# Casting loads on the GpSimd queue, one merged multiply for q and k, a shared phase step and a new program order in a gated linear-attention and GEGLU kernel

## The chip, the cores and the metric

The kernel runs on one core of a Trainium2 chip. The metric is the device time of one execution in microseconds; smaller is better. A run is marked slow when it is over 1.5% above the fastest run of the same kernel, else fast, and ratios are the mean time of one kernel's fast runs over the mean time of the other's fast runs of the same rounds, so they are not quite the ratio of the medians that are quoted beside them. The runs were made on several chips of the same kind. The kernel before took 258 us on some of them and 261 to 264 us on others. A ratio from one chip is not compared finely with a ratio from another.

## The reference

Four sequences of 768 steps with 8 heads of width 48 go through a recurrence with a complex decay; its real output, 3072 rows of 384, goes through a gated feed-forward block.

```python
mag = np.sqrt(a_re * a_re + a_im * a_im)
scale = np.minimum(mag, 0.999) / (mag + 1e-06)
a_re_n, a_im_n = (a_re * scale, a_im * scale)
for t in range(S):
    # ar, ai: a_re_n and a_im_n of step t
    new_re = ar * S_re - ai * S_im
    new_im = ar * S_im + ai * S_re
    S_re, S_im = new_re + k_t v_t^T, new_im        # 48 x 48 per head (shortened)
    y[:, :, t] = q_t S_re
# ...
out = (gelu(x @ w_gate) * (x @ w_val)) @ w_out      # x: y as 3072 x 384, d_ff 1536 (shortened)
```

## The kernel before

The kernel works on 24 chunks of 128 steps. Three chunks are a "unit", which is half of a sequence; a unit's a_re and a_im (576 KB each) give logarithm and angle of the decay, TensorE sums them along time, ScalarE makes exponentials (`E`) and sines (`sn`) of the sums. VectorE multiplies q and k by the exponentials (`qe`, `ke`) and by cosine and sine (`qp`, `kp`) into a tile `pair`. This is transposed either on TensorE with a copy (`tp`, `tps`) or by a transposing DMA (`tpd`). Scores, state and output follow, then the feed-forward part: two up products `g` and `v`, Gelu, product, down product `fo`.

The order is written by hand: a plan of some thousand words is executed as program order on every engine. A word such as `ldk3=1` is "load k of chunk 3 into buffer 1". The parts that the change and the argument touch:

```python
        q=bufs("q", 6, [128, H, D], fp32), k=bufs("k", 6, [128, H, D], fp32),
        v=bufs("v", 6, [128, H, D], fp32),
# ...
    def load(nm, i, slot):
        t = take(nm, (nm, i), slot)
        src = DRAM[nm]
        if nm in ("q", "k", "v"):
            b, c = divmod(i, NCH)
            nc.sync.dma_start(out=t, in_=src[b, :, c * L:(c + 1) * L, :].transpose([1, 0, 2]))
            return
# ... a_re and a_im: also on the sync queue
    def load_weight(nm, after):          # "ldwo@v4": not before v of chunk 4 has arrived
        t, src = WEIGHTS[nm]
        if after:
            a = T[after]
            # ...
            nc.gpsimd.tensor_copy(out=t[:, 0, 0:1], in_=a)
        nc.gpsimd.dma_start(out=t, in_=src.rearrange("(c p) f -> p c f", p=128))
# ...
    def ph(c, slot, **_):
        # ...
        nc.vector.tensor_scalar(out=t[:, 1], in0=T["cumt", c],
                                scalar1=TURN / (2.0 * PI), scalar2=None, op0=ALU.mult)
        nc.vector.tensor_scalar(out=t[:, 0], in0=t[:, 1],
                                scalar1=TURN / 4.0, scalar2=None, op0=ALU.add)
# ...
    def ke(c, slot, **_):
        nc.vector.tensor_tensor(out=take("ke", ("ke", c), slot), in0=T["k", c], in1=T["e", c][:, 1],
                                op=ALU.mult)
    # qe: the same with q and T["e", c][:, 0]
    def vb(c, slot, **_):
        nc.gpsimd.tensor_copy(out=take("vb", ("vb", c), slot), in_=T["v", c])
# ...
    def tpd(c, hg, slot, **_):           # transposing DMA of half a pair tile; xtd is the same for x
        src = T["pair", c][:, hg * 4:(hg + 1) * 4].rearrange("p h i s d -> p (h i s d)")
        nc.sync.dma_start_transpose(out=take("tps", ("tps", c, hg), slot), in_=src)
```

## Time and profile before

| | before |
|---|---|
| median of the timed runs | 258.99 us |
| span of the profiled run (slow) | 263.8 us |
| first Gelu, which is the start of the feed-forward part | 44.12 us |
| TensorE busy | 212.6 us |

The prediction shows the busy times, a table by stretches and the pieces of the chain around the output weights. Three more views of the same profile are needed. The first is the share of each engine in the chain that ended last, where "DMA" is time in which the chain waited for a transfer. (The chain is followed back from the last instruction, at each step to what released it.)

```profile
PE 49%; DMA 18%; ACT 16%; DVE 9%; issue 2%; POOL 0%; SPq 0%; DVEq 0%; ACTq 0%
```

The second is the span cut in two at the first Gelu; the columns are the stretch and its length, then the busy time of PE, PEld, DVE, ACT and POOL with the number of instructions, the clock granted to TensorE, the share of the DMA engines and GB/s.

```profile
0.00:44.12 44.12, 18.56 (x157) 12.58 (x158) 28.69 (x49) 29.17 (x38) 10.23 (x34) 0.88 1.01 211
44.12:263.80 219.68, 194.01 (x2878) 163.21 (x2874) 168.86 (x297) 136.60 (x211) 14.53 (x22) 0.97 0.77 143
```

TensorE, the busiest engine, was idle for 44.12 - 18.56 = 25.6 us ahead of the first Gelu and for 219.68 - 194.01 = 25.7 us after it. This run was a slow one. A fast run of 258.66 us has a span of some 256.9 us (the profiled runs' times are 1.7 to 1.8 us above their spans), so with the same busy time the idle time is 256.9 - 212.6 = 44.3 us, and about 19 us of it come after the first Gelu. That is an estimate: it takes the opening to be the same in a fast run, as a fast run of one of the experiments (b_ph, first Gelu at 44.16 us) suggests.

The third is the loads of q, k and v whose transfer fell in the opening (source, queue, number, size of one, median us from issue to landing):

```profile
k<-in_k_dram SPq DMA_DIRECT2D x6, 192.0 KB, 4.0
...
q<-in_q_dram SPq DMA_DIRECT2D x4, 192.0 KB, 3.8
v<-in_v_dram SPq DMA_DIRECT2D x4, 192.0 KB, 8.5
```

There are 14 of them. Over the whole run the landing times to compare with later are these:

```profile
aim<-in_a_im_dram SPq DMA_DIRECT2D x2, 576.0 KB, 7.3
...
tps<-pair SPq DMA_TRANSPOSE x26, 3.8
```

### The profile page before, as it was taken

Reading aid. Unit: us, or ns where it says so; the run is one execution under the profiler, and the core shown is the slowest. Engines: PE = TensorE matmul, PEld = TensorE weight load, DVE = VectorE, ACT = ScalarE, POOL = GpSimd, SP = SyncE. Lnnn points to the kernel's source line nnn. Section 1 sums busy time; section 2 is a strip of 40 time slices with the busy share of each in tenths; the row PEclk is TensorE's granted clock in tenths of the full one; section 3 lists DMA queues with packets and bytes.
Section 4 is the critical chain, followed back from the end, with each engine's and each line's share of the span. In section 5 each row is a group of like instructions: output and inputs, shape, how many; then the busy total and the mean of one; then the engine's idle time right before and its main releaser. Section 6 shows DMA issues by size and latency. Waiting matters only on the chain.

```text
span 263.8 us, 7255 instructions
## 1 busy us (share of the span) xinstructions
PE 212.6 (81%) x3031; PEld 175.8 (67%) x3031; DVE 197.6 (75%) x346; ACT 165.8 (63%) x248; POOL 24.8 (9%) x56
## 2 busy tenths in 40 slices
PE   0043678991974989978897898999998999899994
PEld 0021268991542779755787788986667978888962
DVE  4671897976399699999994676789999966854441
ACT  3859738466299576999962333989999523332500
POOL 8100202120000012100020001000100000000000
PEclk9999759998698699999999999999999999999999
DMA  7999998999199999489899999299913968861102
GB/s 215 268 211 205 188 208 172 178 190 171 44 198 232 183 215 191 106 174 211 175 142 170 175 162 188 59 171 219 141 46 103 151 117 193 108 58 47 47 31 89
DMA packets 156017, 40.61 MB, mean 154 GB/s; under 512 B 146512, under 2 KB 155216, under 8 KB 155984
## 3 DMA queue, kind: packets, MB, share of 16 engines
q1 hardware_dynamic: 153632, 36.62, 72.8%
q0 software_dynamic: 2352, 3.54, 7.9%
q8 instruction: 23, 0.38, 0.6%
q14 instruction: 10, 0.08, 0.1%
HBM read 30.67 MB, written 4.72 MB: 134 GB/s over the span
## 4 chain that ended last, share of the span: by engine, by line
PE 49%; DMA 18%; ACT 16%; DVE 9%; issue 2%; POOL 0%; SPq 0%; DVEq 0%; ACTq 0%
PE bank L404 23%; PE bank L427 14%; DMA tps<-pair 10%; DMA wo<-in_moe_w_out_dram 5%; PE bank L289 5%; PE bank L356 3%; ACT e L299 3%; ACT th L278 3%; ACT L445 2%; ACT e L300 2%; PE bank L342 2%; DMA v<-in_v_dram 2%; ACT cs L311 2%; DVE pair L326 2%; ACT tps L212 2%
## 5 line engine op out<-in xcount | busy, mean ns | idle before, releaser
L414 ACT ACTIVATE gel<-bank 128x512 bf16<-128x512 f32 x72 | 42.1, 598 | 51.5 <-PE bank L404 36.9
L420 DVE TENSOR_TENSOR h<-bank,gel 128x512 bf16<-128x512 f32 x72 | 48.2, 686 | 12.9 <-PE bank L404 10.8
L404 PE MATMUL bank<-xt,wg 128*128 128x128 bf16 x864 | 57.0, 221 | 0.3 <-DMA xt<-x 0.3
L427 PE MATMUL bank<-wo,h 128*128 128x384 bf16 x288 | 52.3, 334 | 5.3 <-DMA wo<-in_moe_w_out_dram 5.3
L404 PE MATMUL bank<-xt,wv 128*128 128x128 bf16 x864 | 56.2, 219 | 0.4 <-ACT gel L414 0.4
L404 PEld LDWEIGHTS <-wg 128*128 128x128 bf16 x864 | 51.0, 99 | 1.4 <-issue 0.7
L404 PEld LDWEIGHTS <-wv 128*128 128x128 bf16 x864 | 50.2, 98 | 0.8 <-issue 0.5
L427 PEld LDWEIGHTS <-h 128*128 128x128 bf16 x288 | 27.5, 100 | 22.4 <-DMA wo<-in_moe_w_out_dram 5.4
L359 DVE TENSOR_TENSOR ssb<-bank,tri 128x512 bf16<-128x512 f32 x48 | 32.3, 684 | 11.9 <-PE bank L356 11.7
L323 POOL CAST vb<-v 128x384 bf16<-128x384 f32 x24 | 15.3, 642 | 161.3 <-DMA v<-in_v_dram 101.5
L356 PE MATMUL bank<-tps 128*128 128x128 bf16 x192 | 18.9, 225 | 7.2 <-DMA tps<-pair 5.0
L311 ACT ACTIVATE cs<-ph 128x768 bf16<-128x768 int16 x24 | 19.4, 848 | 4.7 <-DVE ph L306 4.6
L289 PEld LDWEIGHTS <-cum 128*128 128x128 bf16 x36 | 4.5, 124 | 25.5 <-issue 22.9
L356 PEld LDWEIGHTS <-tps 128*128 128x128 bf16 x192 | 12.2, 100 | 10.9 <-DMA tps<-pair 5.8
L445 ACT ACT_TABLE_LOAD x14 | 18.0, 1283 | 1.0 <-PEq L471 0.8
L304 DVE TENSOR_SCALAR ph<-bank 128x384 int32<-128x384 f32 x24 | 13.3, 552 | 7.1 <-PE bank L289 7.1
L289 PE MATMUL bank<-lx,cum 128*128 128x384 bf16 x18 | 4.7, 422 | 16.7 <-DVE lx L275 16.7
L372 PE MATMUL bank<-vb,ssb 128*128 128x48 bf16 x192 | 14.9, 183 | 1.5 <-DVE ssb L359 1.5
L342 PE MATMUL bank<-ident,pair 128*128 128x128 bf16 x176 | 14.1, 234 | 2.1 <-DVE pair L326 2.1
L326 DVE TENSOR_TENSOR pair<-ke,cs 128x768 bf16<-128x768 bf16 x24 | 12.9, 553 | 2.5 <-DMA tps<-pair 2.5
L212 DVE COPY o<-bank 128x384 f32<-128x384 f32 x10 | 5.6, 557 | 12.1 <-PE bank L427 12.1
L299 ACT ACTIVATE e<-bank 128x384 bf16<-128x384 f32 x24 | 12.6, 527 | 3.0 <-PE bank L289 2.9
(70 smaller groups left out, 298.1 us busy)
## 6 DMA issues: line engine op xcount, KB each, us to landing
k<-in_k_dram SPq DMA_DIRECT2D x24, 192.0 KB, 3.8
q<-in_q_dram SPq DMA_DIRECT2D x24, 192.0 KB, 3.7
v<-in_v_dram SPq DMA_DIRECT2D x24, 192.0 KB, 4.1
out_dram<-o SPq DMA_DIRECT2D x24, 192.0 KB, 2.1
are<-in_a_re_dram SPq DMA_DIRECT2D x18, 192.0 KB, 3.7
aim<-in_a_im_dram SPq DMA_DIRECT2D x18, 192.0 KB, 3.8
are<-in_a_re_dram SPq DMA_DIRECT2D x2, 576.0 KB, 5.2
aim<-in_a_im_dram SPq DMA_DIRECT2D x2, 576.0 KB, 7.3
```

Of the source, the lines that this page charges most:

```text
L289: nc.tensor.matmul(ps, mat, xin[:, :, c2, :], start=(n == 0), stop=(n == len(srcs) - 1))
L299: act(out=e[:, 1], in_=T["cum", c], func=AF.Exp, scale=-0.5)
L311: act(out=take("cs", ("cs", c), slot).rearrange("p s h d -> p (s h d)"), in_=lo[:, :, 0], func=AF.Sin, scale=2.0 * PI / TURN)
L326: nc.vector.tensor_tensor(out=T["pair", c][:, :, i, :, 0:D], in0=e.unsqueeze(2).to_broadcast([128, H, 2, D]), in1=T["cs", c].rearrange("p ...
L342: nc.tensor.transpose(ps[:, 2 * hi + i, :], T["pair", c][:, hg * 4 + hi, i], ident)
L356: nc.tensor.matmul(ps[:, hi, :], t[:, 2 * hi + 1, :], t[:, 2 * hi, :], start=True, stop=True)
L359: nc.vector.tensor_tensor(out=take("ssb", ("ssb", c, hg), slot), in0=T["sc", c, hg], in1=tri.unsqueeze(1).to_broadcast([128, 4, 128]), op= ...
L404: nc.tensor.matmul(ps[:, fi * L:(fi + 1) * L], w[:, i, fc * 128:(fc + 1) * 128], T["xt", c][:, i, :], start=(i == 0), stop=(i == NDM - 1))
L414: act(out=take("gel", ("gel", c, f), slot).rearrange("p a t -> p (a t)"), in_=T["g", c, f], func=AF.Gelu)
L420: nc.vector.tensor_tensor(out=T["h", c][:, f * FW:(f + 1) * FW, :].rearrange("p a t -> p (a t)"), in0=T["v", c, f], in1=T["gel", c, f].rea ...
L427: nc.tensor.matmul(ps, T["h", c][:, fc, :], wo_sb[:, fc, :], start=(fc == 0), stop=(fc == NFF - 1))
L445: nc.scalar.preload_act_table_set(TABLES[word[4:]])
```

## The change

The intent is to take work from VectorE, which was full in part of the middle. q, k and v are cast to bf16 by the DMA itself, so that the multiply by the decay runs on bf16 operands, and q and k share one tile and one multiply. The first half of the phase step can run on ScalarE. GpSimd's casts of v go away. The order is new as well: the plan is rewritten from end to end, with five contiguous units instead of two, three units instead of two that take the other form of the logarithm step (SQUARES in the kernel), and more transposing DMAs (36 of pairs for 26, 17 of x for 15).

```diff
-FAST = (0, 1,)
+FAST = (0, 1, 2, 3, 4,)
-        q=bufs("q", 6, [128, H, D], fp32), k=bufs("k", 6, [128, H, D], fp32),
-        v=bufs("v", 6, [128, H, D], fp32),
+        qk=bufs("qk", 8, [128, 2, H, D], bf16), v=bufs("v", 12, [128, H, D], bf16),
...
-            nc.sync.dma_start(out=t, in_=src[b, :, c * L:(c + 1) * L, :].transpose([1, 0, 2]))
+            for n, a in enumerate(src):                  # src: (q, k) or (v,)
+                nc.gpsimd.dma_start(out=t[:, n] if nm == "qk" else t,
+                                    in_=a[b, :, c * L:(c + 1) * L, :].transpose([1, 0, 2]))
...
-    def load_weight(nm, after):
-        ...                                             # the wait for another tile
+    def load_weight(nm):                                # the weights wait for nothing
...
+        if eng == "A":                                  # ph, 14 of 24 times
+            act(out=t[:, 1], in_=T["cumt", c], func=AF.Copy, scale=TURN / (2.0 * PI))
...
-    ke, qe (two multiplies, fp32 input), vb (cast of v on GpSimd)
+    def qk(c, slot, **_):
+        nc.vector.tensor_tensor(out=take("qke", ("qke", c), slot), in0=T["qk", c], in1=T["e", c],
+                                op=ALU.mult)
```

(The lines with "ke, qe" and the comments are shortened; the plan's diff is left out.)

## The prediction

> **What bounds the kernel now.** I read the page's busy shares first, then busy time by stretch, then the chain that ended last, then the groups and DMA issues. The profiled run is of the slow kind (263.8 us of span, granted clock 0.955; the timed runs have a median of 258.99), so I use it for durations and order, and take some microseconds off absolute times.
>
> ```profile
> PE 212.6 (81%) x3031; PEld 175.8 (67%) x3031; DVE 197.6 (75%) x346; ACT 165.8 (63%) x248; POOL 24.8 (9%) x56
> ```
>
> TensorE is the busiest engine, VectorE second, and POOL nearly free. The stretches (span, then busy PE, PEld, DVE, ACT, POOL, clock, DMA share, GB/s) say where TensorE is not fed:
>
> ```profile
> 0.00:12.00 12.00, 0.00 (x0) 0.10 (x1) 5.99 (x10) 7.86 (x7) 6.85 (x28) 1.00 0.93 245
> 12.00:30.00 18.00, 9.05 (x35) 4.35 (x35) 10.27 (x16) 12.82 (x21) 1.55 (x3) 0.91 1.06 208
> 44.00:66.00 22.00, 15.90 (x323) 15.52 (x321) 17.25 (x30) 13.11 (x19) 3.25 (x5) 0.94 1.04 180
> 66.00:90.00 24.00, 18.95 (x141) 11.33 (x142) 16.66 (x30) 17.63 (x27) 0.51 (x1) 0.78 0.81 165
> 90.00:132.00 42.00, 37.21 (x570) 31.69 (x569) 41.07 (x74) 37.04 (x52) 5.32 (x9) 0.99 0.88 178
> 170.00:200.00 30.00, 30.00 (x351) 22.22 (x348) 28.51 (x52) 28.29 (x44) 1.69 (x2) 1.00 0.79 142
> 230.00:264.00 34.00, 30.16 (x434) 25.24 (x431) 14.91 (x24) 8.49 (x15) 0.00 (x0) 1.00 0.25 53
> ```
>
> Three kinds of time: an opening of some 44 us in which the feed-forward matmuls can't start; stretches where VectorE is full (41.07 of 42 us); and an end where TensorE alone works. The DMA engines are at 0.8 to 1.06 until about 200 us. In order of time the chain has these pieces:
>
> ```profile
> 46.78 5.09 DMA v<-in_v_dram
> 51.92 0.72 POOL vb L323
> ...
> 53.40 12.48 DMA wo<-in_moe_w_out_dram
> 65.93 4.04 PE bank L427 x12
> ```
>
> So the output weights were held until chunk 4's v had landed and been cast; TensorE then stood still for 5 us and ran its first output group cold (4.04 us, where later ones take 1.95).
>
> **What the Trainium skill says.** "VectorE: DVE Perf Modes", section on the perf-mode tier table: a tensor_tensor runs at 2x only if every tensor is 16-bit in SBUF, else at 1x. The trace agrees: half the elements with an fp32 input take the same time as twice as many in bf16.
>
> ```profile
> L319 DVE TENSOR_TENSOR qe<-q,e 128x384 bf16<-128x384 f32 x24 | 12.7, 551 | 1.9 <-DMA q<-in_q_dram 1.7 <-ACT e L300 0.2
> L326 DVE TENSOR_TENSOR pair<-ke,cs 128x768 bf16<-128x768 bf16 x24 | 12.9, 553 | 2.5 <-DMA tps<-pair 2.5
> ```
>
> "DMA: Bandwidth & Descriptors", section "SWDGE vs HWDGE vs iDMA": a DMA that casts must come from GpSimd, whose cores write its descriptors. The trace has three such DMAs, the weights; they kept POOL 0.79 to 1.06 us each. Same page, "Issuing engines are not separate DMA queues": all queues share the 16 DMA engines. The trace agrees: the two queues' shares add to 1.06 in 12 to 30 us. "SBUF — State Buffer", section "SBUF: two separate sides": VectorE in a two-port mode locks GpSimd out, so descriptors wait. Nothing in this trace shows that; only the short second phase step and the clamp are candidates, so I give it little.
>
> **The change part by part.** "Spacing" below is start to start when back to back, read from the timeline.
>
> VectorE. The 48 multiplies of k and q at 0.465 us spacing (22.3 us) become 24 of 128x768 in bf16, taken at the 0.465 us of the pair multiply: minus 11.1. Of 24 phase steps 14 go to ScalarE: minus about 8. The new plan has 7 transposed-tile copies instead of 15 (0.6 us): minus 4.8. More output, state and x copies (44 for 30, 0.465 us): plus 6.5. The rest (x transposes, logarithm units) cancels. VectorE falls from 187 to about 170 us of spacings.
>
> ScalarE. 14 phase steps at 0.37 us: plus 5.2. One more table load: plus 1.3. Two tile copies (0.9) and 12 narrow copies (0.37) fewer: minus 6.2. It stays at 154 us.
>
> TensorE. 80 transposes of pairs and 6 of x go (0.056 us each): minus 4.8. Five instead of two (batch, half) units use the three-matmul cumulative sums: 18 more at 0.163 us, plus 2.9. From some 192 to 190 us: no relief of the busiest engine itself.
>
> POOL. The 24 casts (15.3 us) go; 72 DMA issues of about 0.95 us come, about 68 us. Harmless: there is nothing else in its order.
>
> DMA. Packets stay as many for q, k, v (1024 per load), each reading 192 bytes and writing 96. In the trace's packet records a plain 192-byte packet takes 15 ns (median), 576 bytes 29, 1536 bytes 66: about 8 ns fixed plus 0.038 per byte. The casting packets took 78 ns for 1536 bytes read and 248 for 6144: about 21 ns fixed. Estimate for a casting 192-byte packet: 28 ns, so 1.85 us instead of 1.0 per load and engine. That is 72 x 0.85 = 61 us of added DMA time. Ten more pair transposes at 1.0 to 1.8 us each (18 to 28 ns per packet): plus 10 to 18. The three more contiguous units: minus 6. DMA time rises from about 214 to 280 us per engine, which only fits into 255 because two queues overlap somewhat (the shares above 1). It is the second tight resource.
>
> The path. In the new order the first Gelu comes after two units' sums, exponentials and sines, chunks 0 to 11. Summing spacings in program order, ScalarE has 49.9 us of work up to there, 27.8 before. Before it came at 44.12 us. After: the value weights load from the first microsecond and share the DMA engines with a_re and a_im, so I put the first a_im at about 12 us instead of 9. Walking ScalarE's order from there, with the table loads and the waits for cumulative sums, gives about 68 to 70 us. But more is behind TensorE then: 170.5 us of its spacings are left instead of 180.4, with 133 us of VectorE (163 before) and 104.5 of ScalarE (126 before). Before, 180.4 us of TensorE's work took about 218 us, 1.21 times: the 12.5 us weights, and a stretch of 58 to 95 us in which 18 us of TensorE's work took 37. The weights now come earlier, and with VectorE at 78% of TensorE instead of 90% the factor should fall to about 1.09, which is what the before shows in its fed part (131 to 200 us: 65 us of work in 69, and 54 in 60 at the end). 69 + 1.09 x 170.5 = 255; 1.8 us between span and time, minus some 2 for the slow state: **255 us**.
>
> **The rivals.** (1) *VectorE relief passes through*: 18 us less on an engine that is full at 90 to 132 us, and the feed-forward work denser; factor 1.05 or an opening of 62 us, 243 to 248. For it: 41.07 of 42 us. Against: TensorE's sum hardly falls and the end is TensorE's alone. (2) *The casting DMAs become the bound*: with 28 ns per packet, loads and transposes of 66 to 208 us add to about 180 us of DMA time in 142 us; q, k, v and the transposes come late, and TensorE waits on tiles: 265 to 280. For it: the fixed 21 ns, DMA shares near 1 now. Against: overlap of queues, eight q/k and twelve v buffers instead of six, the sync queue freed of loads ahead of transposes (they are 10% of the chain now), and an estimate from only two sizes. (3) *The longer opening eats the gain*: 24 us later to the first Gelu against 10 us less TensorE work left and a better factor: 257 to 262. This is close to my sum, so the sign is not safe.
>
> **Range and chances.** The sum gives 255. Opening plus or minus 5, factor 1.05 to 1.12 (plus or minus 6), DMA up to plus 20: 242 to 274, skewed upward. Faster by over 2% is under 253.8, slower over 264.2. I give faster 0.42, since a plan reordered this widely was presumably made to gain; same 0.33; slower 0.25.
>
> **What would show it.** The merged multiply at about 0.55 us mean, x24; VectorE near 178 us busy, ScalarE near 166, TensorE near 210; the first Gelu at 65 to 72 us; POOL's issues near 0.95 us each; the wait of TensorE on the output weights gone; the casting queue's packets at 28 ns each and DMA shares over 1 up to 200 us. The prediction is wrong upward if waits on q, k, v loads or transposes fill the middle of the chain, or POOL's issues take several microseconds; downward if the first Gelu comes before 62 us or TensorE after it has under 10 us of idle time.

## The result, and the profile after

| | before | after |
|---|---|---|
| median (range) | 258.66 us (258.01 to 262.86) | 276.18 us (275.68 to 278.24) |
| ratio of fast runs | | 1.0717, 95% interval 1.0648 to 1.0787 |
| first Gelu | 44.12 us | 75.87 us |

The changed kernel is 7% slower. A repeat beside the experiments (after_again) gave 274.8 us and 1.067 (1.0608 to 1.0731).

> The kernel after, unchanged, so that the next runs can be read against it on one chip: 1.06 to 1.08 times the kernel before.

First the busy times and the chain's shares of the changed kernel's page:

```profile
PE 210.2 (77%) x2963; PEld 175.3 (64%) x2963; DVE 182.4 (67%) x311; ACT 166.2 (61%) x249; POOL 72.0 (26%) x101
...
PE 52%; DMA 32%; DVE 9%; ACT 3%; issue 2%; SPq 1%; DVEq 0%; ACTq 0%
```

VectorE lost 15 us of busy time and TensorE 2, yet the span grew. Waits for transfers are now 32% of the chain instead of 18%. The same span cut at the first Gelu:

```profile
0.00:75.87 75.87, 29.69 (x260) 19.68 (x260) 41.89 (x69) 51.40 (x68) 43.80 (x69) 0.84 1.68 183
75.87:274.00 198.13, 180.48 (x2703) 155.65 (x2703) 140.54 (x242) 114.76 (x181) 28.18 (x32) 0.98 0.87 114
```

This is the most useful view. TensorE's idle time ahead of the first Gelu is 75.87 - 29.69 = 46.2 us, where it was 25.6. After it, it is 198.13 - 180.48 = 17.7 us, about what I estimate for a fast run before (19). The account closes: 20.6 us more idle time in the opening, 1 us less after it, 2.4 us less busy time, 17 us in all, which is 274.0 - 256.9. The repeat has 44.7 and 16.2 us. **By this count all of the added idle time lies in the opening.** That says where the time is and not yet why: the experiments show that idle time taken out of the opening can come back after it. What went on there on the casting queue (first line: queue, packets, MB, share; then the loads as before):

```profile
q0 software_dynamic: 43952, 7.47, 123.6%
...
v<-in_v_dram POOLq DMA_DIRECT2D x14, 96.0 KB, 9.8
qk<-in_q_dram POOLq DMA_DIRECT2D x13, 96.0 KB, 9.5
qk<-in_k_dram POOLq DMA_DIRECT2D x13, 96.0 KB, 8.8
```

Forty casting loads were under way before the first Gelu. The program asks for 16 of them up to that place (q and k of five chunks, v of six); the other 24 ran ahead, since eight q/k and twelve v buffers stood free and GpSimd had nothing else to do. The a_im loads beside them and, later, the transposing DMAs landed later than before:

```profile
aim<-in_a_im_dram SPq DMA_DIRECT2D x5, 576.0 KB, 13.7
...
tps<-pair SPq DMA_TRANSPOSE x36, 4.6
```

And in the chain, in order of time, with start and length:

```profile
3.17 15.61 DMA aim<-in_a_im_dram
...
24.60 15.66 DMA aim<-in_a_im_dram
...
68.20 7.79 DMA tps<-pair
...
146.91 8.57 DMA tps<-pair
```

The first two are the opening's two long waits for a_im. The others are single waits for a transposed pair that are well above the median. After the first Gelu TensorE itself stood still for 14.0 us until a transposed pair or x had landed, 5.3 us before the change; the 5.3 us for the output weights are gone. Two groups tell of the intended gain and of the new loads (busy us and mean ns, then idle time ahead of them and what ended it):

```profile
L215 POOL DMA_DIRECT2D qk<-in_q_dram x24 | 21.7, 905 | 54.9 <-DVE qke L312 50.3 <-DMA v<-in_v_dram 4.3 <-issue 0.2
...
L312 DVE TENSOR_TENSOR qke<-qk,e 128x768 bf16<-128x768 bf16 x24 | 13.1, 548 | 0.0
```

The merged multiply takes 548 ns and does what two of 551 ns did. GpSimd waits 50.3 us for q/k buffers (`qke` is their reader): the loads are ahead of the program as far as the buffers let them. In this profile no multiply waits for q or k.

### The profile page after: what moved, and what is told of

It is laid out like the page before. It is cut to its first block, busy times and chain, and to the rows that moved or that the text cites. A ratio compares the mean times of both kernels' runs of the same rounds, so it can differ in the third digit from the quotient of the medians.

```text
span 274.0 us, 7060 instructions
## 1 busy us (share of the span) xinstructions
PE 210.2 (77%) x2963; PEld 175.3 (64%) x2963; DVE 182.4 (67%) x311; ACT 166.2 (61%) x249; POOL 72.0 (26%) x101
## 4 chain that ended last, share of the span: by engine, by line
PE 52%; DMA 32%; DVE 9%; ACT 3%; issue 2%; SPq 1%; DVEq 0%; ACTq 0%
PE bank L389 28%; DMA aim<-in_a_im_dram 11%; PE bank L412 11%; DMA tps<-pair 10%; DMA xt<-x 9%; PE bank L280 5%; PE bank L341 3%; PE bank L327 2%; DVE z L240 1%; PE bank L357 1%; DVE ssb L344 1%; PE bank L355 1%; ACT L430 1%; DVE pair L318 1%; DMA out_dram<-o 1%
## 5 line engine op out<-in xcount | busy, mean ns | idle before, releaser
L389 PE MATMUL bank<-xt,wv 128*128 128x128 bf16 x864 | 58.2, 222 | 0.0
L215 POOL DMA_DIRECT2D qk<-in_q_dram x24 | 21.7, 905 | 54.9 <-DVE qke L312 50.3
L280 PEld LDWEIGHTS <-cum 128*128 128x128 bf16 x90 | 10.1, 115 | 35.5 <-issue 29.4
L280 PE MATMUL bank<-th,cum 128*128 128x384 bf16 x45 | 11.7, 410 | 27.1 <-ACT th L269 27.1
L215 POOL DMA_DIRECT2D v<-in_v_dram x24 | 21.8, 920 | 35.9 <-PE dwb L362 12.2
L318 DVE TENSOR_TENSOR pair<-qke,cs 128x768 bf16<-128x768 bf16 x48 | 24.4, 550 | 0.3
L215 POOL DMA_DIRECT2D qk<-in_k_dram x24 | 21.9, 913 | 9.2 <-DMA wo<-in_moe_w_out_dram 4.9
L430 ACT ACT_TABLE_LOAD x15 | 19.2, 1283 | 1.0 <-PEq L455 0.8
L240 DVE TENSOR_TENSOR z<-aim,z 128x1152 f32<-128x1152 f32 x8 | 10.8, 1352 | 12.5 <-DMA aim<-in_a_im_dram 11.2
L357 PE MATMUL bank<-v,ssb 128*128 128x48 bf16 x192 | 15.7, 186 | 2.5 <-DVE ssb L344 2.5
L327 PE MATMUL bank<-ident,pair 128*128 128x128 bf16 x96 | 8.3, 250 | 12.1 <-DVE pair L318 12.1
## 6 DMA issues: line engine op xcount, KB each, us to landing
aim<-in_a_im_dram SPq DMA_DIRECT2D x5, 576.0 KB, 13.7
```

Of the source, the lines that this page charges most:

```text
L215: nc.gpsimd.dma_start(out=t[:, n] if nm == "qk" else t, in_=a[b, :, c * L:(c + 1) * L, :].transpose([1, 0, 2]))
L280: nc.tensor.matmul(ps, mat, xin[:, :, c2, :], start=(n == 0), stop=(n == len(srcs) - 1))
L318: nc.vector.tensor_tensor(out=pair[:, :, i, :, 0:D], in0=T["qke", c][:, i].unsqueeze(2).to_broadcast([128, H, 2, D]), in1=T["cs", c].rearr ...
L357: nc.tensor.matmul(ys, T["ssb", c, hg][:, hi, :], T["v", c][:, h, :], start=first, stop=True)
L389: nc.tensor.matmul(ps[:, fi * L:(fi + 1) * L], w[:, i, fc * 128:(fc + 1) * 128], T["xt", c][:, i, :], start=(i == 0), stop=(i == NDM - 1))
L430: nc.scalar.preload_act_table_set(TABLES[word[4:]])
```

## The experiments

For most of them I give the TensorE idle time ahead of and after the first Gelu, worked out as above from the cut of each profile.

| kernel | median us | first Gelu | q/k/v loads before it | idle before | idle after | idle in all |
|---|---|---|---|---|---|---|
| after | 276.2 | 75.87 | 40 | 46.2 | 17.7 | 63.8 |
| after_again | 274.8 | 76.29 | 40 | 44.7 | 16.2 | 60.8 |
| e_gate | 277.2 | 66.83 | 27 | 36.0 | 27.6 | 63.5 |
| e_gate_r | 277.2 | 66.64 | 27 | 35.6 | 23.2 | 58.8 |
| e_bigdesc | 277.6 | 81.03 | 40 | 51.9 | 15.2 | 67.1 |
| e_bigdesc_r | 279.4 | 81.89 | 40 | 50.8 | 14.7 | 65.5 |
| e_gate_bigdesc | 276.2 | 67.92 | 31 | 36.9 | 25.4 | 62.3 |
| e_pace40 | 273.5 | 66.78 | 21 | 38.4 | 23.6 | 62.0 |
| e_pace20 | 272.3 | 67.31 | 18 | 36.0 | 20.5 | 56.5 |
| e_hw32 | 268.3 | 71.14 | 16 | 40.2 | 15.5 | 55.7 |
| e_gate_hw32 | 270.0 | 67.77 | 16 | 37.2 | 18.9 | 56.0 |

These are single profiles, and a few matmul records can be missing, so differences of 2 or 3 us say little; the changed kernel and its repeat differ by 3.

### The opening: weights that wait (e_gate, repeated as e_gate_r)

In the changed kernel the three weight matrices (1,152 KB each) load without a gate from the first microsecond. The experiment holds each until an a_im load has landed. GpSimd works in program order, so the gates hold back the casting loads behind them as well: 27 were issued before the first Gelu instead of 40.

```diff
-... la1=1 ldwv z0 ... ln1=0 ldqk0=0 ...           tp1.1=5 ldwg     ... qk4=4 ldwo ...
+... la1=1 z0      ... ln1=0 ldqk0=0 ldwv@aim1 ... tp1.1=5 ldwg@aim2 ... qk4=4 ldwo@aim3 ...
```

> The kernel after, with the three weight loads held back again: value weights until the second a_im has landed, gate weights until the third, output weights until the fourth. Theory A (ungated weights on the gpsimd queue take the DMA engines from a_re and a_im in the opening): first two a_im land at about 9 to 10 us instead of 15.7 and 18.8, the third well before 40, the first Gelu at 60 to 67 us instead of 75.9, time 260 to 267. Theory B (the loss is in the middle, where bursts of casting loads delay the transposing DMAs): the opening may shorten, but tiles still come late and the time stays above 270. Theory C (casting packets at 29 ns bound the DMA engines): 273 to 278, as only the order of loads changes.

Measured: 277.16 us, ratio 1.0501 (1.0394 to 1.0609). The first Gelu came 9 us earlier, but the time did not follow:

```profile
0.00:66.83 66.83, 30.85 (x252) 21.37 (x253) 41.88 (x69) 50.92 (x69) 35.28 (x59) 0.80 1.35 177
66.83:276.40 209.57, 182.01 (x2714) 155.60 (x2711) 140.51 (x242) 115.05 (x181) 39.53 (x45) 0.98 1.05 117
```

The landings of theory A came about: the first a_im was used at 10.05 us instead of 15.73, the third unit's at 31.4 instead of 40.28. Its time did not, and the time lies where both B and C had it. The opening's idle time fell by 10 us and the rest's rose by 10. The chain's new piece right at the place where the gated weights and the held-back casting loads now land is this wait:

```profile
59.38 9.35 DMA tps<-pair
```

So the ungated weights, with the casting loads behind them, do make the opening late, but holding them back mostly moved the wait. On another chip the repeat gave the same time.

> Repeat of the kernel with the gated weights, so that it stands on the same chip as the pair: 1.04 to 1.06, first Gelu near 67 us.

Measured: 277.24 us, 1.0544 (1.0466 to 1.0622), first Gelu at 66.64 us. The changed kernel did not run on these two chips. By the times and by the idle time in all (63.5 and 58.8 us against 63.8 and 60.8) the gates gain little or nothing; by the ratios (1.050 and 1.054 against 1.072 and 1.067) they would gain some 1.5%. The record does not settle it.

### Only the casting loads undone (e_hw32, and with the gates e_gate_hw32)

q, k and v come as fp32 on the sync queue again, into eight staging tiles, and GpSimd casts them into the same bf16 tiles. Order, merged multiply and phase step stay.

```diff
-                nc.gpsimd.dma_start(out=t[:, n] if nm == "qk" else t, in_=...)
+                f = SB["f"][len(FN) % 8]
+                nc.sync.dma_start(out=f, in_=...)
+                nc.gpsimd.tensor_copy(out=t[:, n] if nm == "qk" else t, in_=f)
```

> The kernel after, with only the casting DMAs undone: q, k, v come as fp32 on the sync queue into eight staging tiles and POOL casts them (0.64 us each) into the same bf16 tiles; multiplies and order stay. Theory B (bursts of the second queue delay transposes): transposes of pairs land in about 3.8 us instead of 4.6 and those of x in 2.9 instead of 3.6, time 262 to 268 even with ungated weights. Theory C (cost of casting packets): DMA time per engine falls by some 60 us and the time to about 262. Theory D (the new order itself is slow, whatever brings the loads): 272 to 280, and sync now blocks transposes behind loads.

> Both edits: gated weights, and q, k, v as fp32 on the sync queue with POOL casts, in the new order. If theories A and B hold and their losses add: 252 to 258. If only A holds: like the gated kernel. If the order itself is slow (D): above 265.

Measured: 268.32 us and 1.0136 (1.0003 to 1.027) without gates, 269.99 us and 1.0251 (1.0172 to 1.0329) with them. Both ran on the chip of e_gate, where the kernel before took 263.77 us. With the gates on both sides only the way of q, k and v differs (cast by the DMA on the GpSimd queue, or fp32 on the sync queue with staging tiles and a GpSimd cast): 277.16 against 269.99 us. So **on the same chip the casting loads cost this order some 7 us**. TensorE's own waits show where. These are for transposed pairs and x in the whole span (total us, times, longest), with the casting loads and then without:

```profile
PE bank L344 <- DMA tps<-pair: 16.0, 10, 4.2
PE bank L392 <- DMA xt<-x: 5.7, 4, 3.2
...
PE bank L348 <- DMA tps<-pair: 6.6, 6, 2.0
PE bank L396 <- DMA xt<-x: 2.2, 1, 2.2
```

That is 21.7 against 8.8 us. What is left, 1.4 to 2.5% in time there (the interval of the first begins at 1.0003), I put to the order and the other parts; the 252 to 258 us of theories A and B together were missed. The profile without gates:

```profile
0.00:71.14 71.14, 30.98 (x252) 21.58 (x253) 41.83 (x69) 51.27 (x69) 20.74 (x45) 0.80 0.89 183
71.14:266.60 195.46, 179.97 (x2714) 153.92 (x2711) 143.12 (x242) 114.42 (x181) 35.72 (x56) 0.99 0.82 156
```

```profile
f<-in_v_dram SPq DMA_DIRECT2D x6, 192.0 KB, 4.7
...
f<-in_q_dram SPq DMA_DIRECT2D x5, 192.0 KB, 5.5
f<-in_k_dram SPq DMA_DIRECT2D x5, 192.0 KB, 5.0
```

The opening's idle time falls here and the rest's does not rise, which among the variants with casting loads only e_pace20 below comes near. Only the 16 loads that the program asks for go before the first Gelu, as the sync queue carries them in program order with everything else and there are just eight staging tiles. Transposed pairs land in 3.3 us (median) instead of 4.6 (4.2 in the changed kernel's repeat).

### The casting loads alone, in the old order (b_cast, b_cast2)

```diff
-        q=bufs("q", 6, [128, H, D], fp32), k=..., v=bufs("v", 6, [128, H, D], fp32),
+        q=bufs("q", 6, [128, H, D], bf16), k=..., v=bufs("v", 14, [128, H, D], bf16),
-            nc.sync.dma_start(out=t, in_=...)
+            nc.gpsimd.dma_start(out=t, in_=...)
```

> The kernel before in its old order and with its gated weights, but q, k, v by casting DMAs of the gpsimd queue (no POOL casts, bf16 multiplies of k and q at half the time). Theory C: slower by 8 to 20 us (267 to 279). Theory B: slower by 2 to 8 us from 130 us on, where the transposing DMAs are. Theory A (only weights and run-ahead in the opening matter): equal or faster, 252 to 259, as VectorE has some 9 us less to do.

b_cast had a mistake of mine: with 12 v buffers taken in turn, one was overwritten before its last reader in program order. The result was wrong, and its 260.37 us (0.991) are not used. The mended kernel:

> The earlier run of the old order with casting DMAs, with its mistake mended (a v buffer was reused before its last reader in program order): result correct. Time as there, 0.98 to 1.0 times before: in the old order, with transposes on TensorE while most loads move, the casts cost nothing and VectorE's relief shows a little.

Measured: 259.27 us beside 258.1, ratio 1.0069 (1.0022 to 1.0115), and a correct result. VectorE fell from 197.6 to 188.8 us busy, and the first Gelu stayed at 43.95 us. In the old order, with six q and k buffers and gated weights, the casting loads cost next to nothing and gain nothing. Nineteen of them were issued before the first Gelu, where 14 loads were, and transposed pairs landed in 4.4 us instead of 3.8. So landings as late as the changed kernel's need not cost time by themselves.

### Is it the queue or the cast? (e_sw32)

The loads stay on the GpSimd queue but do not cast; GpSimd casts afterwards, four loads behind.

> The kernel after, with q, k, v still on the gpsimd queue, but as fp32 without a cast; POOL casts them (four loads behind its issues). Separates the cast in the DMA from the second queue. If the casting packets (29 ns instead of 15) are what delays the transposes: like the kernel with fp32 on the sync queue, 1.01 to 1.03 times before. If it is that loads on a second queue share the DMA engines with the transposes whatever their type: 1.05 to 1.08, landings of pair transposes 4.3 us or more.

Measured: 287.8 us (282.22 to 293.52), three of the four runs slow, so no ratio. GpSimd's casts now wait in order for landings between its load issues, so the time is confounded. One reading is usable: transposed pairs landed in 4.3 us and x in 3.7, like the changed kernel's 4.6 and 3.6, with no cast in any of these DMAs. It also had no short packets on that queue: 6,960 packets in all, where the changed kernel has 77,232. This points to the second stream of loads as what delays the transposes, and not to the cast; it is one profile, and of a slow run.

### Is it the many short packets? (e_bigdesc, repeated as e_bigdesc_r)

```diff
-                                    in_=a[b, :, c * L:(c + 1) * L, :].transpose([1, 0, 2]))
+                rows = a[b].rearrange("h s d -> (h s d)").rearrange("(c p f) -> c p f", p=128, f=DM)[c]
+                nc.gpsimd.dma_start(out=(...).rearrange("p h d -> p (h d)"), in_=rows)
```

> The changed kernel with one edit: each q, k or v load reads 128 contiguous rows of 1,536 bytes instead of 1,024 pieces of 192 bytes. Same bytes, same queue, same casting, same places in the program, same waits; the rows are the wrong ones, so the result is wrong on purpose. Theory P (the many short casting packets of the second queue delay the transposing DMAs and the a_re and a_im loads that share the 16 DMA engines with them): ratio to the kernel before 1.00 to 1.03, transposed pairs land in about 3.3 us (4.6 in the changed kernel), xt in about 2.5 us (3.6), DMA under 27% of the chain. Rival O (what delays them is that loads run ahead on a second queue at all, or that queue's bytes): ratio stays 1.05 to 1.075, landings stay near 4.6 and 3.6 us, DMA near 32% of the chain.

> Repeat of the kernel with the long rows, on the same chip as the pair: 1.04 to 1.06, first Gelu near 81 us, the rest near 192 us.

Measured: 277.56 us, 1.0542 (1.0421 to 1.0663), and 279.36 us, 1.061 (1.0525 to 1.0694), wrong results as intended. Both ratios lie in the rival's range. The landings moved towards theory P (3.8 and 3.9 us for pairs, 2.4 and 2.9 for x; the changed kernel had 4.6 and 4.2, 3.6 and 3.7), DMA was 31% and 26% of the chain, and the idle time after the first Gelu fell a little, to 15.2 us. But GpSimd issues such a load in 542 to 560 ns instead of 905 to 920, the loads ran ahead faster still, and the first Gelu slipped to 81.03 us. Short packets seem to have a share in the late transposes, but lifting them did not bring the time back.

### Both at once (e_gate_bigdesc), and the phase step (e_phV)

> The changed kernel with both edits at once: the three weight loads held until the a_im loads of units 1, 2 and 3 have landed, and the q, k and v loads reading 128 contiguous rows of 1,536 bytes (wrong rows, so a wrong result on purpose). Theory (two separate costs of the second queue that add: its bytes delay the a_im loads of the opening, its many short packets delay the transposing DMAs later): first Gelu at 65 to 70 us as with the gates alone, the part after it 192 to 198 us as with the long rows alone, ratio 1.00 to 1.03. Rival (the order has another limit that takes over whenever one of the two is lifted): part after the first Gelu 203 us or more, ratio 1.04 to 1.055.

Measured: 276.23 us, 1.0489 (1.0411 to 1.0567). The theory of two costs that add has fallen; the rival's line was met. The opening is as short as with the gates alone (67.92 us), and the idle time after it is as long (25.4 us). On this one chip, with long rows in both, the gates took the median from 279.36 to 276.23 us; with gates in both, the long rows took it from 277.24 to 276.23. The trace shows what took over. The four transposed pairs of 55 to 92 us landed this late (us from issue to landing), and these were the q, k and v loads of 56 to 74 us:

```profile
DMA to landing us min/median/max: 12.8/14.8/16.2
```

```profile
qk<-in_k_dram POOLq DMA_DIRECT2D x5, 96.0 KB, 9.9
qk<-in_q_dram POOLq DMA_DIRECT2D x4, 96.0 KB, 10.6
v<-in_v_dram POOLq DMA_DIRECT2D x3, 96.0 KB, 10.9
```

Twelve casting loads, held back behind the output weights on the GpSimd queue, came as one burst around two transposes on which TensorE stood waiting. That led to the theory that was tested last.

> The changed kernel with all 24 first phase multiplies on VectorE again (14 had gone to ScalarE), nothing else touched. Neither engine sets the end of the changed kernel by my reading of its chain (ScalarE 3%, VectorE 9%), so the ratio to the kernel before stays 1.06 to 1.075. If the 7 us that the change puts on ScalarE matter, it falls below 1.055.

e_phV puts all 24 first phase multiplies on VectorE again. Measured: 275.38 us, 1.0434 (1.0371 to 1.0497). The expectation was missed in its ratio, but I do not read a gain from it: the kernel before took 264.23 us on this chip, and 275.38 us is what the changed kernel takes on the others (274.8 and 276.2). No run of the changed kernel on that chip settles it, so whether the 7 us on ScalarE matter stays open. The first Gelu stayed at 75.5 us.

### Loads held to the pace of the program (e_pace40, e_pace20)

On top of e_gate, one small GpSimd copy ahead of most casting loads reads a tile that the program writes some 40, or some 20, steps earlier. Queue, order, bytes and packets stay.

```diff
+            elif word.startswith("pace@"):
+                ...
+                nc.gpsimd.tensor_copy(out=pace_t, in_=src)      # ahead of ldqk and ldv words
```

> The kernel with gated weights (277.2 us on two chips) with one addition: ahead of 42 of the 48 places where casting loads are issued, GpSimd copies one element of a tile that the program writes some 40 steps (about 10 us) earlier, so that no load can start before the engines have come that far. Queue, order, bytes and packets of the loads stay. Theory R (loads that run ahead in bursts delay the transposing DMAs): median 264 to 271 us, transposed pairs land in under 4.0 us, transposing DMAs under 18% of the chain. Rival (it is the share of the engines that the casting loads take, whenever they come, or the order itself): 273 to 279 us. A third way: loads come too late, and waits on q, k or v stand in the chain.

> The same with a lead of some 20 steps (about 5 us). Theory R: as with 40, or a little better for the transposing DMAs, 262 to 272 us, if the loads still come in time. Rival: 273 to 279 us. If the lead is too short, waits for q, k or v appear in the chain and the time is above that with 40.

Measured: 273.5 us, 1.0529 (1.0439 to 1.0619), and 272.29 us, 1.0485 (1.0377 to 1.0592). The first is in the rival's range, at its lower end; the second is 0.3 us above the theory's. Both are below e_gate's 277.2 us of two other chips, but their ratios hardly differ from e_gate's 1.050 and 1.054. Transposed pairs landed in 4.8 and 4.3 us, and transposing DMAs took 21% and 18% of the chain, where theory R had under 4.0 us and under 18%. No wait for q, k or v stands in either chain. The profile with the short lead:

```profile
0.00:67.31 67.31, 31.30 (x254) 21.69 (x255) 40.86 (x69) 50.94 (x68) 27.93 (x58) 0.80 1.19 175
67.31:270.80 203.49, 182.95 (x2712) 156.81 (x2710) 140.65 (x242) 114.71 (x181) 55.04 (x91) 0.97 1.13 121
```

With 18 loads before the first Gelu the idle time is 36.0 + 20.5 = 56.5 us, which is that of the kernels without casting loads, though the median stays 2 to 4 us above theirs, on another chip. So running ahead may explain a part of the 7 us; the ratios do not show it, and how large a part it is is not settled.

### The transposes on TensorE (e_pe)

The 39 transposing DMAs ahead of the last load were done on TensorE, with a copy on VectorE or ScalarE each.

> The kernel after with casting DMAs as they are, but the 39 transposing DMAs that stand before the last load are done on TensorE instead (about 15 us more of TensorE, some 18 us more of copies on VectorE). Theory B (transposes delayed by the casting loads): waits of the chain on tps and xt of some 50 us vanish and the time falls to 262 to 270 although TensorE has more to do, 1.02 to 1.045 times before. If the waits are harmless, or the casting loads bound the kernel by their own lateness: 278 to 292, 1.07 or more.

Measured: 304.65 us, 1.1827 (1.1775 to 1.1878), above both ranges. DMA fell from 31% of the chain (after_again, same chip) to 11%, but the time rose by some 30 us:

```profile
PE 65%; DVE 12%; DMA 11%; ACT 7%; issue 2%; SPq 1%; DVEq 0%; ACTq 0%
```

TensorE now waits for those copies and they for TensorE, at places where nothing else was put between them. In this order the waits for transfers are cheaper than that.

### Single parts in the old order (b_ph, b_wo, b_cast_wo_ph)

> The kernel before with one part of the change alone: for the odd chunks the first of the two phase multiplies runs on ScalarE instead of VectorE, no other line touched. Twelve of them leave VectorE (about 6 us of its busy time) and come to ScalarE (about 6 us more). Theory: neither engine sets the end in this order, so the ratio is 0.99 to 1.01. Rival: ScalarE is 16% of the chain of waits of the kernel before, and what it gains lands on that chain: 1.01 to 1.03.

Measured: 263.72 us beside 263.08, ratio 1.0053 (0.9965 to 1.0141): no effect to be seen of twelve phase multiplies on ScalarE.

> The kernel before with the output weights requested earlier, behind the arrival of the v of chunk 3 instead of chunk 4. The chain of waits of the kernel before has a wait for those weights. If that wait is worth what it seems to be, the ratio is 0.985 to 0.995 and the wait is gone from the chain; the rival is that the earlier bytes delay the q and k loads beside them by as much: 0.995 to 1.01.

```diff
-... ldwo@v4 ...
+... ldv3=3 ldwo@v3 ...        (five plan lines earlier)
```

Measured: 262.75 us, 0.9983 (0.9887 to 1.0078). The wait for the output weights is gone from the chain and nothing came of it: in its place the chain has a wait of 12.64 us for a load of q, from 45.38 us on, as the rival had it (the profile is of a slow run). A wait of 12 us in the chain was worth less than the 1% or so that this run can resolve.

> The kernel before in its own order with three parts at once: q, k and v as bf16 by casting DMAs of the gpsimd queue (alone 1.007), the output weights requested behind the v of chunk 3, and the first phase multiply of the odd chunks on ScalarE. If the parts add up to anything, 0.975 to 0.995; if the casting loads and the earlier weights only crowd each other, 1.00 to 1.02.

Measured: 268.52 us, 1.0274 (1.0216 to 1.0332). The three parts, 1.007 (on another chip), 0.998 and 1.005 alone, do not add up but make 2.7%. Why they crowd each other I did not pursue. No version with a correct result beat the kernel before by a clear margin.

## Why the prediction was wrong

The time was predicted as 255 us and is 276.2. By its own steps:

- **The sizes of the instructions held.** Merged multiply 548 ns (0.55 predicted), twice the elements in the time of one fp32 multiply, as "VectorE: DVE Perf Modes" of the Trainium skill has it in its perf-mode tier table; TensorE 210.2 us and ScalarE 166.2 (210 and 166); VectorE 182.4, 4 us above the 178 expected; packet times summed over the queues 300 us per engine (109.4% of the span), where 280 were expected; GpSimd's issue 905 to 920 ns (0.95), with no sign of a lock-out by VectorE. TensorE's wait for the output weights is gone from the chain.
- **The opening failed.** "I put the first a_im at about 12 us instead of 9" measured 15.73 us (the start of its first use), and a_im of the third unit was first used at 40.28 us. The first Gelu came at 75.87 us instead of 69: 6.9 us. The step allowed for the weights as the only other traffic, and for too little of that: without casting loads but with ungated weights (e_hw32) the first a_im was used at 14.60 us, with gates as well at 8.92. And it missed the 40 casting loads, 24 of them ahead of need, because the step on GpSimd had called their issues "Harmless: there is nothing else in its order". That was the error: with an almost free GpSimd, more buffers, and a queue of their own, nothing held them back. Without casting loads (e_hw32) the third unit's a_im was used at 29.1 us and the first Gelu came at 71.14; with the weights gated, and the casting loads held back behind them, it came at 66.8. Both lie inside the predicted 65 to 72.
- **The factor failed.** 170.5 us of TensorE's spacings were left, and they took 198.1 us: 1.16 times instead of 1.09, or 12.3 us. Before it was 1.21. With 180.5 us of TensorE busy after the first Gelu, the factor 1.09 left room for 5 us of idle time; there were 17.7. The wait for weights and VectorE's congestion, which the step took away, were replaced by waits for transposing DMAs: TensorE stood 14.0 us on them, and eight such waits of 4 to 9 us stand in the chain after the first Gelu. The sign that the prediction gave for being wrong upward, waits on transposes in the middle of the chain, is what came. The casting loads are only a part of this: without them (e_hw32) the stretch still took 195.4 us, 1.15 times, with 8.8 us of waits for transposes, and no variant got under 14.7 us of idle time there. Why the new order needs the rest stays open. The two mis-sized terms make 6.9 + 12.3 = 19.2 us, and 1.7 us from span to time in place of the 0 that I netted against the slow state: 255 + 19 + 2 = 276.
- **Against the time before, though, it is the opening that counts.** TensorE's idle time after the first Gelu is no larger than before; I had booked a gain there that did not come, to pay for a longer opening. Rival 3, a longer opening that eats the gain, named this mechanism and gave it 257 to 262 us. Of the 20.6 us more idle time in the opening some 10 are the traffic (36 us of idle time are left in the variants with gates), and about 10 stayed in every variant. I put these to the order, which has 51 us of ScalarE's work ahead of the first Gelu instead of 29, and only 11 us more of TensorE's; this is read from the profile and no run tested it.
- **Rival 2 had the size and half of the mechanism.** Transposes came late, as it said. But it priced the packets at 28 ns each (29 measured, the median) and added them up to engine time. In the trace packets of the casting queue overlap: 8,460 of them passed between 19 and 25 us, 529 per engine in 6 us, or 11.3 ns each, and the queue's share for that stretch was 259%. In the changed kernel's profile neither TensorE nor VectorE waits for q, k or v; they wait for the transfers beside them. (In e_phV's chain waits for q, k and v take some 16%, all in the opening.) "DMA: Bandwidth & Descriptors" of the Trainium skill says in "Queues, rings and completion order" that each DMA engine takes turns between the queue rows that have work, a packet at a time (its packet is a group of descriptors and need not be what the profile counts as one). The landing times agree with a stream that takes turns with the transposes (3.3 us without it, 4.6 beside it, 16.2 at worst in a burst of long rows), but no run here shows the turns themselves. The argument of mine against rival 2, that the sync queue is freed of loads ahead of transposes, did not hold: with all loads on the sync queue, in program order, transposed pairs landed sooner (3.3 us) than with the loads moved off it (4.6).

What stays open: how the 7 us of the casting loads divide between running ahead, short packets and the mere presence of a second stream (running ahead and short packets, lifted alone, gave little in time), and what in the new order costs the rest. No run put the new order's parts back one by one.

## What to carry to other kernels

Before loads are given a queue and buffers of their own, count how many of them the program needs before its first critical result, and how many could then be under way: what runs ahead shares the DMA engines with what is waited for. Cut the span at the point where the main work starts and compare the busiest engine's idle time on both sides; it told in two lines where the added idle time lay, while the chain showed a dozen waits, and those that were lifted (the output weights in b_wo, a_im in e_gate) did not give their length back. Neither view is a cause: idle time taken out of the opening came back after it in e_gate.

## What the Trainium skill lacked or had wrong

- "DMA: Bandwidth & Descriptors", section "Issuing engines are not separate DMA queues", says that issuing from several engines saves only issue time. It lacks that it can cost: with q, k and v on the second queue transposed pairs landed in 4.6 us (median; 4.2 in the repeat) instead of 3.3 and the 576 KB a_im loads in 13.7 us instead of 6.5 (the changed kernel against e_hw32, which also runs ahead less and does not cast), and the kernel took 7 us longer (277.2 against 270.0 us, one chip, weights gated in both).
- The same page, "Anatomy of one DMA — SWDGE (gpsimd) path", calls descriptor generation small and variable, and does not say how long a load of many pieces keeps GpSimd: here 905 to 920 ns for 1,024 pieces of 192 bytes, 542 to 560 ns for 128 rows of 1,536 bytes.
- No page that I read warns that the packet times in a profile overlap and so may not be added up to engine time: a queue's share was 259% in one stretch, with a median packet of 29 ns and one packet per 11.3 ns and engine.
